# The count behind an order written by a planner: zeros' products booked as two instructions, a drift of the count, and a draw that passes attention products by

## The chip, the cores and the metric

The kernel runs on one core of a Trainium2 chip. The metric is the device time in microseconds of one execution.

## What is computed

Three stages follow each other; shapes are those of the run, all in fp32.

```python
# 1: delta-rule attention, 4 x 8 heads, 768 steps, head size 48
k_n = k / (norm(k) + 1e-6)
for t in range(768):
    y[t] = q[t] @ state
    state = state + beta[t] * outer(k_n[t], v[t] - k_n[t] @ state)
x = y as 3072 x 384
# 2: mixture of 8 experts, 384 -> 1024 -> 384, every token through every expert
P = exp(x @ w_gate - max)
for _ in range(8):
    P /= P.sum(1); P /= P.sum(0); P *= 3072 / 8
x = sum over e of P[:, e] * (relu(x @ w1[e]) @ w2[e])
# 3: a second layer
out = ((x @ w1) * (x @ w2)) @ w3 @ w_out
```

## The kernel before

The sequence is cut into 12 chunks of 64 steps. For each chunk the kernel forms products of the keys among themselves (the Gram matrices, tile `kt`), solves a triangular system on VectorE (`invert`, tiles `asys` and `t`), makes the transform `tt`, and walks from chunk to chunk with the state `st` (`seq`: products with `st`, `kt`, `qt`, `vs`, `u`, `pt`, `kraw`). A chunk has about 11 groups of such small fp32 products on TensorE; most are `quads` of 32 calls of `matmul`, booked with `ins=128` instructions, some are booked with 64. In the text these are the attention products. The result of a chunk goes to DRAM, comes back in another layout, and is split into a high and a low fp32r part, the tile `xr`.

Expert 0 of the mixture (`e0`) runs in the gaps of the attention: per chunk 24 groups of three matmuls with `xr` and 24 with the hidden layer `hA`, each booked with the default `ins=6`. It needs only the chunk's `xr`, of which there are two buffers. The weights of expert 0 lie in `wA`. Once the last chunk's gate logits are there, the eight rounds of normalisation of P run mostly on VectorE (`sinkhorn`). Then come experts 1 to 7 in three passes over the tokens (`unit`, tiles `xT`, `xr`, `wA`, `wS`, `hA`, `hB`); their weights go into the same buffers `wA` as expert 0's, so they can be written only when expert 0's products have read them. The last part is the second layer (`phase_c`).

The program is straight-line code. Its order is not written by hand: `Plan.order` is a list scheduler that runs when the program is built. It keeps a modelled clock `now`, takes the ready operations by priority, and gives each a start and an engine from a table of costs. The order in which it takes them is the order of the engines' queues; the hardware's own waits do the rest.

For TensorE the planner also keeps a model of where its code comes from. `issued` counts the instructions it has booked on TensorE so far, from the `ins` of each operation. In `fetch` the code is taken to come in blocks of `BLOCK = 256` instructions, with boundaries at `PHASE + 256 k` of that count, `PHASE = 193`; a block is taken to be ready `FETCH` microseconds after the first instruction of the block before it has started. `fetch(o, now)` is how long the operation `o` would then have to wait. In the choice (line 272) an operation of TensorE for which this is more than 0.1 us is put aside as `spare`, and the next in the list is looked at; it is taken after all when there is nothing else.

While the first chunk is on its way, TensorE would stand still. `setup` therefore books up to 400 products of zeros (line 497, tile `wz`, `fill=True`), which the planner uses only when nothing else is ready, from `WARM = 20` us of its clock until the first product of expert 0; the rest of them is then dropped. Each is booked with `ins=4`.

All matmuls are recorded in the profile under line 395, the helper `mm`, so they are told apart by their tiles.

Of the kernel before, what the change touches and what calls it, by code (L numbers as in the profile page):

```python
# [1 line left out]

# [75 lines left out]
class Plan:  # L78
# [52 lines left out]
    BLOCK = 256  # L131
    PHASE = 193
    AHEAD_AT = 0
    FETCH = 4.2
    SLOW = .06
    WARM = 20.0
    TURN = (.09, .1)

    def wait_for(self, o, e, pool, now, room):
# [10 lines left out]
    def order(self):  # L150
# [6 lines left out]
        now = 0.0  # L157
# [7 lines left out]
        issued = [3]  # L165
        last = ["e"]
        shared = {"DVE": 0.0, "POOL": 0.0}

        def cost_of(o, e):

            if e != "PE":
                return o.engs[e]
            k = int(now / win)
            if k not in warm:
                i = max(warm, default=-1)
                w = warm.get(i, False)
                while i < k:
                    b = busy.get(i, 0.0) / win
                    w = b >= .38 if w else b >= .7
                    i += 1  # L180
                warm[k] = w
            return (o.engs[e] + turn(o)) * (1.0 if warm[k] else self.COLD)

        def started(i, o, now):

            n = issued[0]
            if i >= n:
                return now + min(i - n, o.ins) / max(1, o.ins) * o.engs["PE"] + max(0, i - n - o.ins) * self.SLOW
            for i0, m, a, b in reversed(stream[-300:]):
                if i0 <= i < i0 + m:  # L190
                    return a + (b - a) * (i - i0) / m
            return 0.0

        def fetch(o, now):

            n = issued[0]
            k = -(-(n - self.PHASE) // self.BLOCK)
            b = self.PHASE + self.BLOCK * k
            ready = started(b - self.BLOCK + self.AHEAD_AT, o, now) + self.FETCH
            if b < n + o.ins:  # L200
                return max(0.0, ready - now - (b - n) / max(1, o.ins) * o.engs["PE"])
            if o.ins >= 16:
                return max(0.0, ready - now - o.engs["PE"] - (b - n - o.ins) * self.SLOW)
            return 0.0

        def turn(o):
            return self.TURN[0] if o.ins >= 16 and last[0] == "e" else self.TURN[1] if o.ins < 16 and last[0] == "a" else 0.0

        def crowded():

            return sum(max(0.0, b - max(a, now - win)) for a, b in lows[-8:]) > self.LOWMAX

        def room(o):
            t = o.est
            need = {}
            for s in o.slots:
                if s.at is not None:
                    continue
                g = s.ring
                if g.fifo and s.seq != g.given + need.get(("f", g), 0):  # L220
                    return None
                n = need.get(g, 0)
                if n >= len(g.free):
                    return None
                if s.cls in g.caps and g.used.get(s.cls, 0) + need.get((g, s.cls), 0) >= g.caps[s.cls]:
                    return None
                t = max(t, g.free[n][0])
                need[g] = n + 1
                need[("f", g)] = need.get(("f", g), 0) + 1
                need[(g, s.cls)] = need.get((g, s.cls), 0) + 1  # L230
            return t

        while pool:
# [4 lines left out]
            full = crowded()  # L238
            taken = set()
            lead = next((o for o in pool if o.fill), None)  # L240
            for o in pool:
                if o.fill and (now < self.WARM or o is not lead):
                    continue
                if o.est > now and len(taken) == len(free):
                    continue
                engs = [e for e in o.engs if free[e] <= now and o.rdy[e] <= now]
                if o.est > now:
                    nxt = o.est if nxt is None else min(nxt, o.est)
                    continue
                if not engs:  # L250
                    for e, t in o.rdy.items():
                        if t > now:
                            nxt = t if nxt is None else min(nxt, t)
                    continue
                t = room(o)
                if t is None:
                    continue
                if t > now:
                    nxt = t if nxt is None else min(nxt, t)
                    continue  # L260
                if len(o.engs) > 1:
                    cost = {x: max(free[x], o.rdy[x], now) + c * self.BIAS.get(x, 1.0) for x, c in o.engs.items()}
                    e = min(cost, key=cost.get)
                    if e not in engs:
                        t = max(free[e], o.rdy[e])
                        nxt = t if nxt is None else min(nxt, t)
                        continue
                else:
                    e = engs[0]
                if self.wait_for(o, e, pool, now, room):  # L270
                    continue
                if o.low and full or e == "PE" and fetch(o, now) > .1:
                    spare = spare or (o, e)
                    continue
                best = (o, e)
                break
            if best is None:
                best = spare
            if best is None:
                later = [t for t in free.values() if t > now] + ([self.WARM] if lead and now < self.WARM else []) + ([nxt] if nxt is not None else [])  # L280
                if not later:
                    raise RuntimeError("no operation can start: " + str([(o.prio, list(o.engs)) for o in pool[:8]]))
                now = min(later)
                continue
            o, e = best
# [14 lines left out]
            if e == "PE":  # L300
                late = fetch(o, now)
                end += late
                stream.append((issued[0], o.ins, now + late, end))
                last[0] = "a" if o.ins >= 16 else "e"
                issued[0] += o.ins
# [3 lines left out]
            elif e == "PE":  # L309
                t = now  # L310
                while t < end:
                    k = int(t / win + 1e-9)
# [60 lines left out]
class Kernel:  # L373
# [56 lines left out]
    def setup(self):  # L430
        nc, T, g = self.nc, self.T, self.g
        n = NCH * NG
# [61 lines left out]
        sw = self.psum.new("warm")  # L494
        for _ in range(400):
            g.op({"PE": .107}, lambda e: self.mm(self.ps(sw, 256), T["wz"][:, 0:128], T["wz"][:, 128:384], start=True, stop=True),
                 r=["wz"], w=[sw], ins=4, prio=1e6, fill=True)

    def vsrc(self, c):
        return self.a["v"][c]  # L500
# [1109 lines left out]
```

## Time and profile before

| | |
|---|---|
| median of 3 runs | 2100.17 us (2094.9 to 2104.77) |
| the profiled execution | 2098.94 us, its span 2097.1 us |
| instructions in the span | 40050 |
| TensorE (PE) busy | 2055.3 us, 98% of the span |
| VectorE (DVE), ScalarE (ACT), GpSimd (POOL) busy | 58%, 35%, 38% |
| mean granted clock of TensorE | 0.996 |

Times in the profile are microseconds from the start of the span. PE stands for TensorE's matmuls and PEld for its weight loads, which overlap them. Where a wait is called "issue", the engine waited for nothing that the profile shows. The queue "instruction" is one of the DMA queues of the core. The granted clock is a share of TensorE's full speed.

### The profile page before, as it was taken

The page shows a single profiled execution, that of the slowest core. Times are in us where ns is not written, and L with a number is a line of the kernel's source. Part 1 is how long each engine was busy: PE and PEld are TensorE (multiplying, and loading weights), DVE is VectorE, ACT ScalarE, POOL GpSimd, SP SyncE. Part 2 cuts the span into 40 slices and gives each one's busy share as a digit, 9 for nine tenths or more (in the row PEclk, how much of TensorE's full clock was granted, in tenths as well). Part 3 has the DMA queues.
Part 4 walks back from the last instruction along what each step waited for, and adds up shares of the span by engine and source line. Part 5 has one row for each costly group of instructions (what it writes and reads, how often), then busy time and mean ns, then how long its engine had stood idle before and what let it go on. Part 6 is the DMA issues. An engine that isn't in the chain of part 4 may idle for free.

```text
span 2097.1 us, 40050 instructions
## 1 busy us (share of the span) xinstructions
PE 2055.3 (98%) x16493; PEld 1758.3 (84%) x16493; DVE 1214.1 (58%) x1946; ACT 732.8 (35%) x1437; POOL 790.5 (38%) x851
## 2 busy tenths in 40 slices
PE   7998999999999999999999999999999999999999
PEld 6888888978888888878888888788888888988888
DVE  7889793466444445766666677676667643222222
ACT  6444433234334334323333324233233222222222
POOL 1200101037666667444654444444544534200000
PEclk9999999999999999999999999999999999999999
DMA  6443323256454465766656455655556547410000
GB/s 220 134 133 125 93 82 99 66 208 243 179 215 171 186 231 191 248 214 212 218 178 211 170 169 199 221 210 208 173 187 216 180 121 198 95 44 16 16 21 25
DMA packets 166615, 331.64 MB, mean 158 GB/s; under 512 B 13409, under 2 KB 117793, under 8 KB 154913
## 3 DMA queue, kind: packets, MB, share of 16 engines
q1 hardware_dynamic: 132544, 193.82, 27.3%
q0 software_dynamic: 33888, 135.28, 18.9%
q8 instruction: 129, 2.11, 0.4%
q14 instruction: 54, 0.43, 0.1%
HBM read 235.10 MB, written 93.95 MB: 157 GB/s over the span
## 4 chain that ended last, share of the span: by engine, by line
PE 75%; issue 5%; DMA 2%; POOL 1%; DVE 1%; ACT 0%; SPq 0%; POOLq 0%; DVEq 0%; ACTq 0%
PE b L395 75%; DMA acc<-y_d 1%; DMA rawB<-in_moe_w 1%; POOL wA L406 0%; POOL acc L406 0%; POOL sums L406 0%; DMA w_d<-cv 0%; DVE tmp L406 0%; DVE cv L406 0%; DVE cv L409 0%; DMA ws_d<-wS 0%; POOL wS L406 0%; ACT rt L399 0%; DVE rt L406 0%; DVE xr L406 0%
## 5 line engine op out<-in xcount | busy, mean ns | idle before, releaser
L395 PE MATMUL b<-hA,wA 128*128 128x512 f32 (+1 forms) x2367 | 507.7, 354 | 3.5 <-DVE hA L409 3.5
L395 PEld LDWEIGHTS b<-hA,wA 128*128 128x128 f32 x2367 | 393.6, 190 | 65.6 <-DVE hA L409 4.4
L406 POOL TENSOR_TENSOR acc<-acc,tmp 128x512 f32<-128x512 f32 x252 | 335.6, 1333 | 191.6 <-DVE tmp L406 189.9
L395 PE MATMUL b<-hB,wA 128*128 128x512 f32 x1521 | 386.0, 389 | 0.0
L395 PEld LDWEIGHTS b<-hB,wA 128*128 128x128 f32 x1521 | 285.5, 188 | 59.2
L395 PE MATMUL b<-xr,wA 128*128 128x256 f32 (+1 forms) x1620 | 329.8, 337 | 1.2 <-DVE hA L409 0.9
L395 PEld LDWEIGHTS b<-xr,wA 128*128 128x128 f32 x1620 | 252.2, 191 | 33.9 <-DVE hA L409 1.5
L399 ACT ACTIVATE rt<-b 128x512 f32<-128x512 f32 x300 | 178.8, 597 | 263.0 <-PE b L395 257.0
L395 PE MATMUL b<-xT,wA 128*128 128x512 f32 x1008 | 249.9, 389 | 1.3 <-POOL wA L406 1.1
L406 DVE TENSOR_TENSOR b<-b,rt 128x512 f32<-128x512 f32 x252 | 173.2, 695 | 107.1 <-ACT rt L399 75.8
L395 PEld LDWEIGHTS b<-xT,wA 128*128 128x128 f32 x1008 | 189.0, 188 | 41.2 <-POOL wA L406 2.1
L406 POOL TENSOR_TENSOR cv<-cv 128x256 f32<-128x256 f32 (+3 forms) x179 | 131.8, 736 | 205.2 <-DVE cv L1370 107.8
L395 PE MATMUL b<-xT,wS 128*128 128x512 f32 x756 | 199.9, 391 | 1.7 <-ACT rt L399 1.7
L406 DVE TENSOR_TENSOR tmp<-b,pb 128x512 f32<-128x512 f32 x150 | 103.2, 689 | 134.6 <-PE b L395 131.8
L409 DVE SCALAR_TENSOR_TENSOR hA<-b,hA 128x512 fp32r<-128x512 f32 x215 | 144.2, 688 | 61.1 <-ACT hA L935 29.8
L395 PEld LDWEIGHTS b<-xT,wS 128*128 128x128 f32 x756 | 142.2, 188 | 32.4 <-ACT rt L399 2.6
L406 DVE TENSOR_TENSOR rt<-b,rt 128x512 f32<-128x512 f32 x48 | 33.2, 692 | 186.0 <-PE b L395 186.0
L409 DVE SCALAR_TENSOR_TENSOR hB<-b,hB 128x512 fp32r<-128x512 f32 x169 | 114.7, 685 | 32.1 <-ACT hB L1175 31.6
L406 POOL TENSOR_TENSOR wA<-rawB,wA 128x768 fp32r<-128x768 f32 (+1 forms) x49 | 87.9, 1803 | 111.8 <-ACT wA L399 111.3
L406 DVE TENSOR_TENSOR tmp<-b,yr 128x512 f32<-128x512 f32 x102 | 70.2, 689 | 97.3 <-PE b L395 88.2
L1175 ACT ACTIVATE hB<-b 128x512 fp32r<-128x512 f32 x169 | 100.0, 595 | 67.7 <-DVE b L406 65.7
L399 ACT ACTIVATE cv<-cv 128x256 fp32r<-128x256 f32 x72 | 29.1, 404 | 266.7 <-DVE cv L409 266.7
(190 smaller groups left out, 2440.8 us busy)
## 6 DMA issues: line engine op xcount, KB each, us to landing
wA<-wq_d POOLq DMA_DIRECT2D x56, 1536.0 KB, 8.7
wq_d<-wA SPq DMA_DIRECT2D x28, 1536.0 KB, 7.0
wS<-ws_d POOLq DMA_DIRECT2D x56, 512.0 KB, 4.7
rawB<-in_moe_w SPq DMA_DIRECT2D x108, 192.0 KB, 3.3
ws_d<-wS SPq DMA_DIRECT2D x28, 512.0 KB, 6.8
w_d<-cv SPq DMA_DIRECT2D x112, 128.0 KB, 1.7
cvr<-in_w3T SPq DMA_DIRECT2D x32, 256.0 KB, 2.7
wS<-w_d POOLq DMA_DIRECT2D x32, 256.0 KB, 3.5
```

The costliest lines, as they stand in the source:

```text
L395: self.nc.tensor.matmul(*args, skip_group_check=True, **kw)
L399: self.nc.scalar.activation(out=out, in_=in_, func=AF.Copy, **({} if scale is None else {"scale": scale}))
L406: self.E[eng].tensor_tensor(out=out, in0=in0, in1=in1, op=op)
L409: self.nc.vector.scalar_tensor_tensor(out=out, in0=in0, scalar=scalar, in1=in1, op0=op0, op1=op1)
L1175: g.op({"ACT": actb(512)}, lambda e: nc.scalar.activation(out=hv(0), in_=self.ps(s, 512), func=AF.Relu), r=[s], w=[(out, 0, 0)], prio=pe)
```

## The change

Four things change in the planner's model, nothing in the operations themselves. A product of zeros counts as two instructions in place of four. The boundaries are no longer taken at `PHASE + 256 k` of the count alone: one further instruction is assumed for each 450 counted (`DRIFT`). The time that a block is taken to need rises from 4.2 to 4.4 us. And each time an operation of TensorE with 16 or more instructions (an attention product) would be chosen, a number is drawn from a generator with a fixed seed; in one case of twenty it is put aside like one whose code is late. The seed makes the order the same in every build.

```diff
+import random
...
-    FETCH = 4.2
+    FETCH = 4.4
+    DRIFT = 450
     SLOW = .06
     WARM = 20.0
+    SEED = 32
+    PASS_BY = .05
     TURN = (.09, .1)
...
         shared = {"DVE": 0.0, "POOL": 0.0}
+        rng = random.Random(self.SEED)
...
             n = issued[0]
-            k = -(-(n - self.PHASE) // self.BLOCK)
-            b = self.PHASE + self.BLOCK * k
+            extra = n // self.DRIFT
+            k = -(-(n + extra - self.PHASE) // self.BLOCK)
+            b = self.PHASE + self.BLOCK * k - extra
             ready = started(b - self.BLOCK + self.AHEAD_AT, o, now) + self.FETCH
...
-                if o.low and full or e == "PE" and fetch(o, now) > .1:
+                if o.low and full or e == "PE" and (fetch(o, now) > .1 or o.ins >= 16 and rng.random() < self.PASS_BY):
                     spare = spare or (o, e)
                     continue
...
             g.op({"PE": .107}, lambda e: self.mm(self.ps(sw, 256), T["wz"][:, 0:128], T["wz"][:, 128:384], start=True, stop=True),
-                 r=["wz"], w=[sw], ins=4, prio=1e6, fill=True)
+                 r=["wz"], w=[sw], ins=2, prio=1e6, fill=True)
```

## Rows read from the trace of the kernel before

**Rows 1.** Busy time of each engine, page of the profile.

```profile
PE 2055.3 (98%) x16493; PEld 1758.3 (84%) x16493; DVE 1214.1 (58%) x1946; ACT 732.8 (35%) x1437; POOL 790.5 (38%) x851
```

**Rows 2.** Busy us by stretch: window and length, then engines, clock, DMA.

```profile
75.00:355.00 280.00, 264.77 (x6873) 242.03 (x6870) 219.84 (x341) 115.62 (x268) 27.19 (x31) 0.98 0.35 105
355.00:436.00 81.00, 79.86 (x660) 78.66 (x659) 39.82 (x88) 24.04 (x47) 0.95 (x1) 1.00 0.23 70
436.00:2097.10 1661.10, 1648.25 (x7432) 1384.10 (x7430) 893.81 (x1416) 543.36 (x993) 743.64 (x799) 1.00 0.49 169
```

**Rows 3.** PE's waits from 75 to 355 us: total, times, longest.

```profile
PE b L395 <- issue: 9.2, 11, 1.6
```

**Rows 4.** PE's waits before 75 us.

```profile
PE b L395 <- issue: 2.9, 3, 1.2
```

**Rows 5.** PE's waits from 436 us to the end.

```profile
PE b L395 <- ACT rt L399: 4.4, 3, 2.7
PE b L395 <- DVE hA L409: 3.5, 2, 2.0
PE b L395 <- POOL wA L406: 1.1, 1, 1.1
```

**Rows 6.** The queue called instruction, DMA part of the page: packets, MB.

```profile
q8 instruction: 129, 2.11, 0.4%
```

**Rows 7.** Counts between ends of issue waits; PE counts matmuls, PEld loads.

```profile
13.89:39.72 25.83, 22.68 (x510) 18.63 (x510) 24.52 (x47) 21.93 (x73) 1.06 (x1) 1.00 0.58 206
...
210.64:240.21 29.57, 27.89 (x766) 25.46 (x766) 22.50 (x45) 11.24 (x27) 4.78 (x3) 1.00 0.31 91
240.21:245.68 5.47, 4.47 (x127) 4.18 (x128) 5.47 (x6) 4.73 (x11) 0.00 (x0) 0.64 0.48 150
...
13.89:331.25 317.36, 297.22 (x7656) 267.43 (x7655) 268.67 (x421) 148.72 (x364) 37.30 (x29) 0.98 0.38 117
```

**Rows 8.** Single blocks of code, cut at the same place of each.

```profile
35.09:39.72 4.63, 3.99 (x135) 3.61 (x132) 4.17 (x9) 1.07 (x2) 1.06 (x1) 1.00 0.89 278
...
113.12:115.21 2.09, 2.09 (x131) 2.03 (x131) 0.69 (x1) 1.28 (x4) 0.00 (x0) 1.00 0.60 221
...
142.09:145.92 3.83, 2.26 (x128) 1.90 (x127) 3.83 (x3) 2.32 (x7) 0.13 (x1) 1.00 0.45 131
...
302.43:305.92 3.49, 3.07 (x145) 2.72 (x136) 3.49 (x4) 1.08 (x2) 0.00 (x0) 1.00 0.30 76
```

**Rows 9.** The zeros (tile wz) from 15 to 75 us.

```profile
15.00:75.00 60.00, 28.92 (x220) 21.39 (x220) 0.00 (x0) 1.00 0.56 181
```

**Rows 10.** The two stretches at the lower granted clock (0.50).

```profile
146.20:149.60 3.40, 3.40 (x16) 3.40 (x17) 2.12 (x5) 0.83 (x2) 1.37 (x2) 0.50 0.89 258
...
241.80:252.00 10.20, 9.20 (x189) 8.78 (x193) 6.83 (x7) 6.18 (x14) 1.83 (x1) 0.50 0.29 79
```

**Rows 11.** Timeline of PE around 246 us: start, length, product, matmuls.

```profile
240.21 0.33 PE L395 MATMUL b<-vs,tt 64*64 64x48 f32 x6 [1.43 <-issue]
...
246.18 2.29 PE L395 MATMUL b<-xr,wA 128*128 128x256 f32 x9
248.27 2.76 PE L395 MATMUL b<-hA,wA 128*128 128x256 f32 x12
250.96 1.58 PE L395 MATMUL b<-pt,u 64*48 64x64 f32 x64
```

**Rows 12.** Timeline of PE around 332 us, at full clock.

```profile
327.89 0.62 PE L395 MATMUL b<-hA,wA 128*128 128x256 f32 x3
328.44 0.69 PE L395 MATMUL b<-asys,g 32*32 32x32 f32 x32
329.06 1.11 PE L395 MATMUL b<-pt,u 64*48 64x64 f32 x64
...
336.51 1.96 PE L395 MATMUL b<-hA,wA 128*128 128x256 f32 x15
338.40 1.15 PE L395 MATMUL b<-st,kt 48*64 48x48 f32 x64
```

## The prediction

> **What bounds the kernel now.** I begin with the page. PE is busy for 98% of the span, no other computing engine for more than 58% [rows 1]. Then I cut the span into stretches [rows 2]. The reader is to see there that from 75 us on PE is the limit everywhere: in the attention stretch (75 to 355 us) it is idle for 280.00 - 264.77 = 15.2 us, in the rest of expert 0 (355 to 436 us) for 1.1 us, and in everything after 436 us for 12.8 us of 1661. The list of what PE's idle time waited for comes next, stretch by stretch. From 75 to 355 us, 9.2 of the idle microseconds are called "issue": PE waited for nothing that the profile shows, 11 times [rows 3]. Before 75 us there are three more, 2.9 us together [rows 4]. After 436 us there is none; PE waits there for ScalarE, VectorE and GpSimd, 9.0 us in all [rows 5].
>
> What are the issue waits? The queue called "instruction" moved 129 packets and 2.11 MB, 16.4 KB each [rows 6]; PE ran 16493 matmuls and as many weight loads, 32986 instructions, which is 255.7 for each packet [rows 1, 6]. So PE's code comes in blocks of 256. Then I cut the span at the ends of the issue waits and counted matmuls and loads between them [rows 7]: 1020, 1532, 255 are three of the twelve counts, and all twelve are multiples of 256 less a few. From the end of the first wait (13.89 us) to that of the last (331.25 us) it is 15311 = 60 x 256 - 49. Every wait thus stands at the same place of a block, and the few that are missing (one in 312) are instructions of PE's queue that are not matmuls or loads. I read the waits as PE running off the end of a block before the next is there. A block lasts 317.36 / 60 = 5.3 us on average, and those that end in a wait last 3.5 to 5.5 us [rows 7, 8]; one of 2.09 us ended in none [rows 8], so what stood ahead of it counts too.
>
> **The change, part by part.**
>
> *The zeros' count.* 220 products of zeros were run, with 220 matmuls and 220 loads: two instructions each [rows 9]. The planner before booked four, so after the last of them (71 us) its count is 440 too high. In a block of 256 that sets its boundary 72 instructions behind the real one. The uncounted instructions push it on: after 49 of them it is some 120 behind, nearly half a block. The planner before did keep attention products away from boundaries, but from 15 us on from wrong ones. With two, its boundary is the real one less the uncounted instructions.
>
> *The drift.* One instruction in 450 books 15311 / 450 = 34 of those 49. The boundary is then at most some 15 instructions out by 331 us; an attention product of 128 takes 1.1 us [rows 12], so that is 0.13 us. Both edits together make the planner's boundaries right for the first time.
>
> *FETCH 4.2 to 4.4.* The planner holds an attention product back when the block would otherwise last less than this. I looked at eleven blocks that end in a wait; four of them stand in rows 7 and 8. They last from 3.49 to 5.47 us, and six of them longer than 4.4, by 2.4 us together: 0.22 us for each of the eleven. So with true boundaries a block that is planned tight still waits some 0.2 us. With 60 blocks of 5.3 us on average against 4.4, I take 16 as tight: 3.5 us stay. Bounds: none stays (0), or as many as now.
>
> *What a removed wait is worth.* Held-back attention leaves PE to expert 0's products; that work has to be done anyhow, and 80 us of it lie behind the attention's end [rows 2], so PE has something to run and each idle microsecond saved between 75 and 355 us brings the end of expert 0 forward by one. The work at 436 us hangs on that end: the next expert's weight tiles come free with its last products. VectorE is busy for 219.84 of the 280 us; if it set the pace of the attention, PE would still do expert 0's products in that time. The first wait (13.9 us, 1.2 us) stays: no zeros come before it. Of the other two before 75 us I count their 1.7 us, as the attention runs alone there. Removable: 9.2 + 1.7 = 10.9 us; less the 3.5 that stay, 7.4 us saved (bounds 0 and 10.9).
>
> *The clock.* In two stretches of the attention the granted clock is 0.50, which is 1.2 GHz in place of 2.4: 146.2 to 149.6 and 241.8 to 252.0 us [rows 10]. Each begins within 1.6 us of the end of an issue wait: the block up to 145.92 us is idle for its last 3.83 - 2.26 = 1.57 us [rows 8], and 1.43 us of waiting end at 240.21 [rows 11]. What they cost, from products at either level: at full clock 15 matmuls of expert 0 hold their place for 1.89 us, 0.126 each [rows 12]; in the slow stretch 9 and 12 take 2.09 and 2.69 us, 0.228 each [rows 11], so 0.45 of each slow us is lost. An attention product (b<-pt,u) takes 1.58 against 1.11 us: 0.30 lost [rows 11, 12]. The long stretch mixes both, with 9.2 us of work in its 10.2: at 0.40 it costs 3.7 us. The short one is nearly all expert 0: 1.5. If the fall follows the wait, both go; but another pause may bring another fall. I take 60% of the 5.2: 3.1 us saved (bounds: 5.2 saved; or as much again lost).
>
> *The draw.* Each time an attention product is the planner's choice it is put off by one turn with chance 1 in 20. By the code a chunk has about 11 such products, some 135 in all, so about 7 are put off, always behind something else that is ready. The work stays; what is added is a change between the two kinds. A single group of 3 expert-0 matmuls between attention products holds its place for 0.55 us where 3 in a row of 15 take 0.38 [rows 12]: 0.17 each, 1.2 us added (bounds 0 and 3; a gain through a luckier order is in the last item).
>
> *The rest of the order.* From 436 us on the same units run, but the planner's clock has shifted, so ties fall otherwise. The waits there are 9.0 us [rows 5]; I take no change, with bounds of 4 either way. The transfers and the other engines' work are the same.
>
> Sum: 2098.94 (the profiled execution; its span is 2097.1, 1.8 less) - 7.4 - 3.1 + 1.2 = 2089.6. The runs' median is 2100.17, 1.2 above the profiled one; I forecast for that median: **2090.8 us**, 0.45% less. A measurement of this kernel tells about 0.5% (10.5 us) from no change, as its three runs span 9.9 us, so the forecast lies next to that edge.
>
> **The rivals.**
>
> *The waits stay, or move (no change).* The boundaries are right, yet held-back attention piles up and runs two products deep right behind the boundary, and the next block is short. For it: a block with a wait starts the next late too (the blocks up to 240.21 and 245.68 both wait [rows 7, 8]), and 5.3 us on average leaves only 0.9 us of room. Against it: most of the 60 blocks have no wait even with wrong boundaries. Time: 2100.2 + 1.2 for the draw, less 0 to 4 of waits: about 2099.
>
> The Trainium skill (Runtime: NRT & Kernel Launch, section Instruction fetch mechanics) says that the sequencer fetches the next 16 KiB page while it runs the current one, and that crossing a boundary is mostly hidden. By that rule the edits would gain nothing, and the time would be that of this rival; the trace disagrees for the attention, with 12.1 us in 14 waits, and agrees after 355 us, where there is none.
>
> *Everything goes (clearly faster).* No wait but the first (-10.9), both slow stretches (-5.2), draws free, 2 us less waiting in the last part: 2100.2 - 18.1 = 2082. For it: slow stretches began behind waits. Against: the planner's price is an average over blocks that differ by 2 us.
>
> *The clock falls more often (slower).* The new order makes other pauses between 75 and 355 us, and the granted clock falls at them. Price 0.40 us for each slow us. Without any clock gain the sum is 2100.2 - 7.4 + 1.2 = 2094; to be slower by 10.5 us it takes 17 us more, 42 us of further slow clock, four stretches as long as the worst now. Against it: 13.6 us in all are slow there, with 14 waits.
>
> **How the numbers follow.** Chances: forecast 0.58 (2083 to 2098, which the edge of 2089.7 cuts nearly in half: faster 0.28, same 0.30); waits stay 0.20 (same); everything goes 0.14 (faster); clock 0.08 (slower). That is faster 0.42, same 0.50, slower 0.08. The range leaves out the slower case and the lower part of "everything goes", and takes in the bounds of the draw and of the last part: 2080 to 2101.
>
> **What the profile after will show.** Right: the issue waits of PE before 355 us fall from 12.1 to about 4.7 us (3.5 and the first); what is left still stands at multiples of 256; the clock is 1.00 from 75 to 355 us but for at most one stretch; expert 0's last product ends 7 to 13 us before 436; the stretch after takes 1661 us as before, give or take 4. Wrong: as many issue waits as now (the boundary or the 4.4 us are not what decides), or the waits gone and the same microseconds found as waits for VectorE or ScalarE (the attention, not PE, set the pace), or more of the span at 0.50.

## The result and the profile after

The changed kernel takes 2076.44 us (median of 4 runs, 2073.56 to 2079.21) against 2097.53 for the kernel before: 0.9896 of it, with a 95% interval of 0.9862 to 0.9931. The forecast was 2090.8 with a range of 2080 to 2101; the gain is 21 us where 9 were forecast, and the time lies under the range. The profiled execution has a span of 2076.4 us.

First the stretches, cut where expert 0's last product ends: at 436.4 us before, at 414.9 us after. The columns are those of [rows 2]; the first fence is of the kernel before, the second of the changed one.

```profile
0.00:436.40 436.40, 407.46 (x9066) 374.61 (x9067) 320.65 (x531) 189.85 (x446) 47.29 (x53) 0.98 0.37 117
436.40:2097.10 1660.70, 1647.85 (x7428) 1383.69 (x7427) 893.41 (x1416) 542.96 (x992) 743.25 (x799) 1.00 0.49 169
```

```profile
0.00:414.90 414.90, 394.38 (x9036) 365.51 (x9037) 317.88 (x534) 190.62 (x447) 48.55 (x51) 1.00 0.39 123
414.90:2076.40 1661.50, 1649.69 (x7428) 1384.33 (x7426) 890.99 (x1414) 542.47 (x992) 743.80 (x799) 1.00 0.49 169
```

The reader is to see that all of the gain lies in the first row. It is 21.5 us shorter, and the rest of the kernel takes 1661.5 us against 1660.7. Of the 21.5 us, 8.4 are idle time of PE (436.4 - 407.46 = 28.9 before, 414.90 - 394.38 = 20.5 after) and 13.1 are busy time, though the same products of attention and of expert 0 run.

Next the stretch before 75 us, of the kernel before and of the changed one, then the attention stretch of [rows 2] and the zeros, both of the changed kernel.

```profile
0.00:75.00 75.00, 62.42 (x1542) 53.51 (x1543) 60.58 (x103) 49.79 (x131) 18.74 (x21) 1.00 0.62 211
```

```profile
0.00:75.00 75.00, 60.28 (x1559) 52.16 (x1560) 58.16 (x101) 47.17 (x123) 23.46 (x23) 0.98 0.58 201
75.00:355.00 280.00, 275.33 (x6997) 255.34 (x6995) 222.58 (x350) 124.05 (x288) 23.71 (x27) 1.00 0.37 112
```

```profile
15.00:75.00 60.00, 24.64 (x189) 17.83 (x186) 0.00 (x0) 0.97 0.50 168
```

From 75 to 355 us PE is idle for 4.7 us where it was for 15.2 [rows 2], and the granted clock is 1.00 where it was 0.98. From 15 to 75 us the zeros take 24.6 us in place of 28.9 [rows 9], but this is not time gained: PE's idle time before 75 us rises from 12.6 to 14.7 us, and the first product of expert 0 starts at 63.1 us where it started at 64.0.

The waits of PE, before 75 us and from 75 to 355 us, as in [rows 3, 4]:

```profile
PE b L401 <- DVE u L412: 2.5, 1, 2.5
PE b L401 <- DVE tt L412: 2.4, 1, 2.4
...
PE b L401 <- issue: 0.8, 1, 0.8
```

```profile
PE b L401 <- issue: 1.9, 2, 1.7
PE b L401 <- ACT u L405: 1.6, 1, 1.6
```

Issue waits are 2.7 us in 3 places where they were 12.1 in 14. The one long one that is left, in the timeline:

```profile
237.89 0.56 PE L401 MATMUL b<-kt 48*64 48x64 f32 x18
240.18 0.86 PE L401 MATMUL b<-kt 48*64 48x64 f32 x44 [1.73 <-issue]
```

One stretch before the end of expert 0 still has the lower clock, 30.7 to 34.1 us, and it begins 1.1 us after the end of a wait of 2.42 us for VectorE:

```profile
29.65 1.16 PE L401 MATMUL b<-tt,xst 64*64 64x64 f32 x64 [2.42 <-DVE tt L412]
30.75 0.40 PE L401 MATMUL b<-wz 128*128 128x256 f16 x1
31.07 1.96 PE L401 MATMUL b<-vs,tt 64*64 64x48 f32 x64
```

```profile
30.70:34.10 3.40, 3.40 (x79) 2.74 (x72) 3.40 (x7) 3.33 (x11) 0.00 (x0) 0.50 0.02 5
```

### The profile page after: what moved, and what is told of

It reads as the page before. It is cut to its first block, busy times and chain, and to the rows that moved or that the text cites. A ratio compares the mean times of both kernels' runs of the same rounds, so it can differ in the third digit from the quotient of the medians.

```text
span 2076.4 us, 39969 instructions
## 1 busy us (share of the span) xinstructions
PE 2044.1 (98%) x16463; PEld 1749.8 (84%) x16463; DVE 1208.9 (58%) x1947; ACT 733.1 (35%) x1438; POOL 792.4 (38%) x849
## 4 chain that ended last, share of the span: by engine, by line
PE 87%; DVE 5%; DMA 5%; issue 1%; POOL 1%; ACT 1%; SPq 0%; POOLq 0%; DVEq 0%; ACTq 0%
PE b L401 87%; DMA acc<-y_d 1%; DMA wo_d<-cv 1%; DVE prod L412 1%; DMA xs_d<-xst 1%; DMA xst<-xs_d 0%; DMA rawB<-in_moe_w 0%; SPq L432 0%; DMA xT<-xs_d 0%; DVE cv L415 0%; POOL acc L412 0%; DVE xs L625 0%; POOL wA L412 0%; DVE hA L415 0%; DMA xf_d<-acc 0%
```

## The experiments

Two theories stood against each other. By the boundary theory the gain comes from code boundaries that the planner now places rightly, so that fewer attention products run into a block that is not there. By the luck theory the draw, or the shaking of the order by any edit, happened on a good order. Each run was timed beside the kernel before, and each ratio is to that; "issue" is the issue waits of PE up to the end of expert 0, "slow" the time up to there at which the granted clock was 0.50 (1.2 GHz), both from the trace of one execution, and the last column is where expert 0's last product ends in it. The traced execution is not always near the median: that of e11 took 2094.56 us, that of e12 2087.52.

| run | median us | ratio, 95% interval | issue us | slow us | expert 0 ends |
|---|---|---|---|---|---|
| before | 2097.53 | 1 | 12.1 | 13.7 | 436.4 |
| changed | 2076.44 | 0.9896 (0.9862 to 0.9931) | 2.7 | 3.4 | 414.9 |
| e1 count alone | 2091.65 | 0.9975 (0.9960 to 0.9989) | 4.2 | 13.7 | 434.2 |
| e2 no draw | 2080.32 | 0.9916 (0.9891 to 0.9941) | 3.7 | 10.2 | 422.0 |
| e3 draw alone | 2094.58 | 0.9984 (0.9967 to 1.0000) | 10.6 | 27.3 | 439.6 |
| e4 planner half a block off | 2088.24 | 0.9947 (0.9925 to 0.9969) | 4.6 | 30.7 | 432.5 |
| e5 count and drift | 2080.04 | 0.9908 (0.9887 to 0.9928) | 4.3 | 6.8 | 420.3 |
| e6 4.4 us alone | 2095.46 | 0.9990 (0.9975 to 1.0005) | 7.3 | 17.1 | 435.2 |
| e7 seed 33 | 2085.12 | 0.9932 (0.9907 to 0.9957) | 2.1 | 13.7 | 426.7 |
| e8 seed 1 | 2096.31 | 0.9996 (0.9980 to 1.0012) | 6.7 | 30.7 | 438.2 |
| e12 seed 2 | 2092.87 | 0.9991 (0.9974 to 1.0008) | 1.5 | 27.3 | 431.5 |
| e17 no draw, drift 312 | 2076.63 | 0.9913 (0.9893 to 0.9932) | 2.4 | 3.4 | 421.1 |
| e18 no draw, 5.2 us | 2114.59 | 1.0095 (1.0072 to 1.0117) | 0.9 | 44.4 | 454.2 |
| e9 changed, code moved 128 | 2078.20 | 0.9912 (0.9889 to 0.9934) | 2.9 | 0 | 416.0 |
| e13 changed, code moved 64 | 2083.81 | 0.9939 (0.9919 to 0.9960) | 4.8 | 17.1 | 423.2 |
| e14 changed, code moved 192 | 2078.11 | 0.9904 (0.9886 to 0.9922) | 2.9 | 6.8 | 416.7 |
| e16 no draw, code moved 128 | 2087.93 | 0.9954 (0.9938 to 0.9970) | 4.9 | 17.1 | 432.1 |
| e11 count and drift, code moved 128 | 2088.58 | 0.9966 (0.9952 to 0.9980) | 8.7 | 17.1 | 434.7 |
| e10 before, code moved 160 | 2085.55 | 0.9957 (0.9942 to 0.9973) | 4.0 | 10.2 | 426.2 |
| e15 before, code moved 48 | 2091.60 | 0.9972 (0.9962 to 0.9982) | 6.6 | 17.1 | 437.1 |

**One edit at a time.** The count alone:

```diff
# kernel before
-                 r=["wz"], w=[sw], ins=4, prio=1e6, fill=True)
+                 r=["wz"], w=[sw], ins=2, prio=1e6, fill=True)
```

> Kernel before with one edit: a product of zeros counts as two instructions. Boundary theory (the gain comes from block boundaries that the planner places rightly): without the drift its boundaries are right to within 10 instructions at 90 us and 49 at 331 us, so most of the gain comes with this edit alone: issue waits of PE before 355 us down from 12.1 to 3 to 6 us, time 2080 to 2088 us. Luck theory (the drawn order is simply a good one; the count decides nothing): 12 us of issue waits as before, time within 6 us of the kernel before.

A quarter of a per cent, 6.6 us: between the two forecasts, just outside the 6 us allowed for no change. The issue waits did fall as the boundary theory said, from 12.1 to 4.2 us. But expert 0 ends only 2 us earlier, since PE's other waits grew by 8.6 us. Waits of this run, before 75 us:

```profile
PE b L395 <- ACT vs L399: 3.8, 1, 3.8
```

The wait of 3.8 us ends at 62.8 us, and at 62.9 the clock falls for 10.2 us. So a removed issue wait is not a gained microsecond by itself; what matters is the sum of PE's pauses and what the clock does after them.

The draw taken out of the changed kernel, and the draw alone put into the kernel before (shown as what it amounts to, without the constants):

```diff
# e2: changed kernel
-    PASS_BY = .05
+    PASS_BY = 0.0
# e3: kernel before
+        rng = random.Random(self.SEED)
...
-                if o.low and full or e == "PE" and fetch(o, now) > .1:
+                if o.low and full or e == "PE" and (fetch(o, now) > .1 or o.ins >= 16 and rng.random() < self.PASS_BY):
```

> Changed kernel without the draw (its chance is 0): count, drift and 4.4 us stay. Boundary theory: issue waits about 3 us, as in the changed kernel with 2.7, and a time within 5 us of it, 2072 to 2082 us. Luck theory: the draw carries the gain, so 2090 us or more.

> Kernel before with the draw alone (same seed, four instructions for a zeros' product, no drift, 4.2 us). Boundary theory: the boundaries are as wrong as before, so issue waits of 10 to 14 us and a time within 6 us of the kernel before. Luck theory: a good part of the gain, 2088 us or less.

Both came out as the boundary theory said: 2080.3 us without the draw, and 2094.6 with nothing but the draw, with 10.6 us of issue waits.

Count and drift without the 4.4 us and the draw, and the 4.4 us alone:

```diff
# e5: changed kernel
-    FETCH = 4.4
+    FETCH = 4.2
-    PASS_BY = .05
+    PASS_BY = 0.0
# e6: kernel before
-    FETCH = 4.2
+    FETCH = 4.4
```

> Changed kernel without the draw and with the time of a block at 4.2 us as before: count and drift alone. If right boundaries carry the gain (boundary theory), issue waits stay at 3 to 5 us and the time at 2078 to 2084 us, near the 2080.3 of the kernel without the draw. If the longer 4.4 us carries it (rate theory: a planner that spaces attention products further apart meets fewer late blocks, wherever it puts the boundaries), issue waits of 6 us or more and 2088 us or more, near the 2091.7 of the count alone.

> Kernel before with the time of a block at 4.4 us, nothing else. Boundary theory: boundaries as wrong as before, 10 us or more of issue waits, 2092 to 2102 us. Rate theory: issue waits fall to about 5 us as in the run with boundaries half a block off (4.55 us), and 2085 to 2090 us.

2080.0 and 2095.5 us: count and drift carry 0.92% by themselves, the 4.4 us nothing that can be told from no change (the interval of e6 holds 1), with or without right boundaries. The issue waits of e6 were a miss: 7.3 us, less than either 10 or the 12.1 of the kernel before, at boundaries as wrong as there. The drift alone, with four instructions for a product of zeros, was not run.

**The place of the boundary, by the planner.** All boundaries of the planner moved by half a block, the draw kept:

```diff
# e4: changed kernel
-    PHASE = 193
+    PHASE = 65
```

> Changed kernel with the first boundary at 65 in place of 193: every boundary of the planner half a block off, all else kept, the draw too. Boundary theory: issue waits come back to 10 us or more before 355 us, each still at a multiple of 256 instructions from the others, and the time to 2092 to 2104 us. Luck theory: another order, so anything from 2076 to 2100 us, and issue waits that bear no relation to the place of the boundary.

Faster than the boundary theory allowed, 2088.2 us, and its issue waits are only 4.6 us. That part of the theory fell: wrong boundaries do not always bring the waits back. The time is 12 us above the changed kernel all the same, and 30.7 us at the lower clock go with it.

**The place of the boundary, by the code.** A cleaner test keeps the order to the letter and moves the real boundaries: tiny products of zeros, two instructions each, go ahead of PE's first product, where it waits for its first keys anyhow.

```diff
     for o in order:
+        if o.eng == "PE":
+            for _ in range(ahead):   # e9, e11, e16: 64; e10: 80; e13: 32; e14: 96; e15: 24
+                self.mm(self.bank[7][0:32, 0:16], self.T["wz"][0:32, 0:32], self.T["wz"][0:32, 128:144], start=True, stop=True)
+            ahead = 0
         o.fn(o.eng)
```

> Changed kernel, its order of operations kept to the letter, with 64 tiny products of zeros (128 instructions) put ahead of PE's first product, where PE waits for its first keys until 4.1 us anyhow. The real boundaries of the code move by half a block against the same order. Boundary theory: issue waits before 355 us rise from 2.7 to 7 us or more, and the time from 2076 to 2084 us or more. Luck theory (this order is good for other reasons): issue waits below 4 us and 2074 to 2080 us.

> The kernel with count and drift alone (2080.0 us, 4.4 us of issue waits), its order kept, and 64 tiny products of zeros (128 instructions) ahead of PE's first: half a block off. Boundary theory: issue waits of 8 us or more and 2086 us or more. Luck theory: 2078 to 2083 us.

> Changed kernel without the draw (2080.3 us, 3.7 us of issue waits), its order kept, with 64 tiny products of zeros (128 instructions) ahead of PE's first. Boundary theory, as the run with count and drift alone bore it out (8.7 us, 2088.6 us): 7 us or more of issue waits and 2086 us or more. If orders with count, drift and 4.4 us are even, below 5 us and 2077 to 2083 us.

For the two orders without a draw the place counts. Count and drift alone lose 8.5 us when the code moves by half a block under them (2080.0 to 2088.6, intervals that do not touch), with issue waits of 8.7 us in place of 4.3; the order without the draw at 4.4 us loses 7.6 (its intervals overlap by a hair), though its issue waits rise only from 3.7 to 4.9 us, short of the 7 expected. That the waits are bound to the code and not to the order shows when matmuls and loads are counted from the start of the span to the end of one wait each, in the kernel before, in e15 (the same order with 48 instructions in front) and in e11 (128 in front):

```profile
0.00:142.08 142.08, 127.52 (x3286) 112.97 (x3287) 119.07 (x193) 76.31 (x192) 21.98 (x25) 1.00 0.50 164
```

```profile
0.00:144.78 144.78, 127.42 (x3286) 111.62 (x3287) 117.77 (x190) 75.77 (x191) 22.50 (x25) 0.98 0.48 157
```

```profile
0.00:142.20 142.20, 124.79 (x3286) 110.94 (x3286) 110.83 (x180) 77.49 (x197) 24.66 (x26) 0.96 0.49 163
```

6573, 6573 and 6572, with the instructions in front counted in. It is so everywhere: all 119 issue waits of the twenty traces end within 6 instructions of 193 + 256 k, if one uncounted instruction is allowed for each 312. The changed kernel's own order, however, lost nothing by half a block, as the luck theory said: 2078.2 us and 2.9 us of waits. Was that a chance?

> Changed kernel, order kept, 32 tiny products of zeros (64 instructions, a quarter of a block) ahead of PE's first. If this order is even enough to run under any boundary (as half a block suggests: 2.9 us of issue waits, 2078.2 us), issue waits stay below 4 us and the time at 2074 to 2081 us. If half a block was a chance, 6 us of waits and 2083 us or more.

> Changed kernel, order kept, 96 tiny products of zeros (192 instructions, three quarters of a block) ahead of PE's first: as for a quarter; 2074 to 2081 us and below 4 us of issue waits if the order is even, 2083 us or more if not.

Three quarters of a block cost nothing either (2078.1), a quarter 7 us (2083.8, intervals that overlap). So this order is more even than the others, but perhaps not under every boundary. And 64 or 96 of the tiny products by themselves cost nothing in this order.

> Kernel before, its order kept to the letter, with 80 tiny products of zeros (160 instructions) ahead of PE's first product. The planner of before put its boundaries 72 (after the last zero) to 121 instructions (at 331 us) behind the real ones, which is 184 to 135 ahead of the next; 160 instructions in front bring the real ones to within 25 of them, without a change of the order. Boundary theory: issue waits fall from 12.1 to 5 us or less, the slow stretches behind them go, and the time falls by 6 to 14 us, to 2084 to 2092 us. Luck theory: no change, 2094 to 2102 us.

> Kernel before, order kept, 24 tiny products of zeros (48 instructions) ahead of PE's first: control for the run with 80, which gained 9 us. The planner's boundaries are now 120 to 169 instructions from the real ones, so further off than before. If the place of the boundary made that gain, nothing is gained here: 10 us or more of issue waits, 2092 to 2104 us. If the tiny products themselves made it (a start in the higher clock, say), 2084 to 2090 us here too.

Moved to where its planner had put the boundaries, the kernel before gains 9 us and keeps 4.0 of 12.1 us of issue waits, with no change of its order. But the control, whose boundaries are further off than in the kernel before, gains 6 us as well, with 6.6 us of issue waits: neither forecast, and its interval overlaps that of e10. The kernel before thus stood at a bad place, and how much of the 9 us is due to the boundaries being right these two runs do not settle.

What right boundaries do shows when the 70 blocks up to the end of expert 0 are timed by that count, their waits taken off. PE runs through 12 of them in less than 3.5 us in the kernel before, and through 1 in the changed one. Over all runs it is 0 to 6 of them where the planner's boundaries are right, 6 in e1, and 9 to 15 where they are wrong, but for e14 with 4. The short blocks go with the boundaries, then; the time does so only in part.

**The draw.** Only the seed changes:

```diff
# e7, e8, e12: changed kernel
-    SEED = 32
+    SEED = 33   # e8: 1; e12: 2
```

> Changed kernel with the next seed, 33. If the draw only shakes the order, the time lies near that without a draw, 2080 us, by 6 us either way, with issue waits of 2 to 5 us. If the seed 32 is a chosen one, this one is slower than it by 4 us or more.

> Changed kernel with seed 1: as for seed 33. Both seeds at 2080 us or above speak for a lucky seed 32; one below 2076 us and one above speaks for plain scatter.

> Changed kernel with seed 2. With seeds 32, 33 and 1 at 2076, 2085 and 2096 us and 2080 us without a draw, plain scatter puts this at 2076 to 2096 us. If it is above 2080 us, the draw costs on average and seed 32 is a fortunate one.

2085.1, 2096.3 and 2092.9 us, against 2080.3 without a draw: seeds 1 and 2 are slower than no draw at all, by 16 and 13 us, and seed 33 by 5, within the intervals. Of four seeds 32 is the only one below the kernel without a draw: a fortunate one. Boundaries that the planner places rightly thus do not make a fast order by themselves, as all four seeds have them. Seed 2 has just 1.5 us of issue waits, fewer than the changed kernel, and is still 16 us slower; the stretches of this run show where:

```profile
75.00:355.00 280.00, 270.62 (x6635) 248.24 (x6634) 218.82 (x340) 115.91 (x271) 20.19 (x21) 0.96 0.31 97
```

The granted clock is 0.96 from 75 to 355 us against 1.00, and 27.3 us up to the end of expert 0 run at 1.2 GHz. That is no single trace's chance: the 11 executions of this order have a mean granted clock of 0.993, the four of the changed kernel 0.9975.

**What is left to set.** The drift that the trace of before shows, one in 312, and a longer time for a block:

```diff
# e17: changed kernel
-    DRIFT = 450
+    DRIFT = 312
-    PASS_BY = .05
+    PASS_BY = 0.0
# e18: changed kernel
-    FETCH = 4.4
+    FETCH = 5.2
-    PASS_BY = .05
+    PASS_BY = 0.0
```

> Changed kernel without the draw (2080.3 us) and with one further instruction for each 312 counted, the share that the trace of before showed, in place of 450. If the 15 instructions of remaining error matter, issue waits fall below 3 us and the time to 2074 to 2079 us. If the rest of the gain is chance of the order, 2076 to 2090 us, not tied to the issue waits but to the time at the lower clock and the other waits.

> Changed kernel without the draw (2080.3 us) and with 5.2 us for a block in place of 4.4. If issue waits still cost what they seem, they fall to the first one alone (below 2 us) and the time by 1 to 3 us, 2076 to 2080 us. If the planner then has to hold attention products for too long, waits for other engines and zeros' products take over: 2084 us or more.

With the traced drift and no draw the kernel takes 2076.6 us, as the changed one does with its draw; the 3.7 us to e2 lie within the intervals. The longer time is the most telling miss. The issue waits go down to the first one, 0.9 us, and the kernel is the slowest of all, 2114.6 us:

```profile
75.00:355.00 280.00, 258.98 (x6246) 237.85 (x6245) 215.84 (x332) 106.76 (x249) 15.28 (x16) 0.93 0.31 95
```

```profile
PE b L401 <- DVE hA L415: 3.7, 5, 1.3
PE b L401 <- DVE tt L412: 3.1, 2, 2.6
...
```

PE is idle for 21 us from 75 to 355 us, none of it for code; it waits mostly for VectorE and ScalarE, and 44.4 us run at the lower clock. I read it as these engines getting the attention's products too late; no run tests that. None of the runs beats the changed kernel by more than the runs differ.

## Why the prediction was wrong

**What bounds the kernel** held: the issue waits stand at code boundaries (the counts of the experiments' section show them at one place of a block in every trace), and the gain ended up entirely before the end of expert 0, with 1661.5 us after it against 1660.7.

**The zeros' count and the drift** carry the change, as said, and together: 0.92% (e5). The drift was described as a small thing worth 0.13 us at the boundary. That is so for the step from 34 to 49 instructions, but without any drift (e1) 0.25% is left. Whether the 49 instructions or another chance order did that, one run does not tell.

**FETCH** was worth nothing alone (e6) nor beside the count and the drift (e2 against e5).

**The step that failed is the sum.** Up to the end of expert 0 it had 9.3 us; the two traces differ by 21.5. (1) "3.5 us stay" was too much: of the 10.9 us called removable 1.9 stayed, and the first wait shrank by 0.4, so the issue waits gave 9.4 us and not 7.4. The price of 0.22 us is an average in which one block has 1.07 of the 2.4 us, the one of 5.47 us that began at the end of a wait [rows 7]; with true boundaries the 16 blocks taken as tight did not wait that much. (2) PE's other idle time between 75 and 355 us, 15.2 - 9.2 = 6.0 us, was put at nothing without a word. It fell to 2.8, so all idle time there fell by 10.5 us. At the start, also put at nothing, little came of it: the zeros took 3.7 us less in all, and PE's idle time other than issue grew by 4.2 us before 75 us. Idle time and zeros together are 12.1 us of the 21.5. (3) "I take 60%" of the slow stretches: from 75 to 355 us both went, and one of 3.4 us came at 30.7. At the prediction's own prices that is 5.2 less 1.4, or 3.8 us between these two traces, against 3.1. (4) The draw's 1.2 us did not show with seed 32 (2076.4 against 2080.3 without, within the intervals); two of the other seeds cost over ten times as much, so what a draw costs is not a few changes between products. These terms make 15.9 us. The other 5.6 us or so are products that take less time in the records at the same granted clock. Changes between attention, zeros and expert 0's two kinds of products do not explain it, with 314 of them before and 319 after; the cause stays open.

**That the clock term came near was luck.** It took the two slow stretches of one execution as belonging to the order. The mean granted clock is known for 97 executions of the kernel before, timed beside the experiments: it goes from 0.993 (median 2102 us) to 1.000 (2089 us) under one and the same order. Their mean is 0.9967, that of the four of the changed kernel 0.9975; at the 13 us that lie between 0.993 and 1.000 this is some 1.5 us, an estimate. At an equal clock the gain is still there: at 0.997 the kernel before takes 2096.3 us (median of 25) and the changed one 2078.2 and 2079.2; at 0.998 it is 2094.9 (of 20) against 2073.6 and 2074.7. So 17 us or more of the 21 are not the clock.

That runs with little slow time (0 to 7 us) end expert 0 by 421.1 us and those with 27 us or more at 431.5 us or later does not show that waits and clock go together: 27 us at 1.2 GHz are 11 to 12 us by themselves at the prices of 0.40 to 0.45, and e12 has 1.5 us of issue waits with 27.3 slow. The rival in which everything goes came nearest, with 2082, but part of that is luck too: it counted 2 us less waiting in the last part, where the time grew by 0.8.

**The rivals.** That the waits stay or move is what happens with seed 1, with 6.7 us of issue waits, and with a block of 5.2 us, where they become waits for other engines. That the clock falls more often is shown by e18, which is slower by 0.95%: issue waits gone, 44.4 us slow. The rule of the Trainium skill that a boundary is mostly hidden (Runtime: NRT & Kernel Launch, section Instruction fetch mechanics) held after expert 0, where no trace has an issue wait, and not in the attention, where moving the code by half a block under an unchanged order cost 8.5 us (e11).

**What stays open.** With the planner's boundaries right (the changed kernel, e2, e5, e7, e8, e10, e12, e17, e18) the issue waits are 0.9 to 6.7 us, 3.1 on average; with wrong ones (the kernel before, e3, e4, e6, e9, e11, e13 to e16) 2.9 to 12.1, 6.5 on average. The times are less clear: right boundaries without a draw gave 2076.6, 2080.0 and 2080.3 us, but 2114.6 with a block of 5.2 us and 2085 to 2096 with three seeds; wrong ones, with the code not moved, 2088.2 (e4) to 2097.5. (e1, right only at first, is in neither group.) About 8 us hang on the place of the boundary itself in two orders (e11, clearly; e16, at the edge of its intervals), though both also run at the lower clock for a while before 60 us, 10.2 us in e11 and 6.8 in e16, where the same orders without the products in front do so not at all (e5) or for 3.4 us (e2); some of the loss may be that. In the changed kernel's order nothing clear hangs on the place: 2 us (e9, e14) and 7 (e13), all within the intervals. The rest goes with the order, by its other waits and slow stretches; that a planner with right boundaries makes better orders is only argued, from three of them, and the seeds speak against it as a rule. The last 4 us of the changed kernel over e2 lie within the intervals.

## What to carry to other kernels

Where a planner orders the instructions, compare its own counts with the trace: two windows cut at the ends of unexplained waits showed the block, and one tile's count the wrong price of two instructions for four. Before the slow stretches of one trace are priced as a gain, compare the granted clock of all executions of the kernel: here 13 us went with it under one and the same order. Ask of all idle time of the bounding engine what becomes of it, not only of the part that the change aims at. Before a random draw is credited, run three other seeds and no draw.

## What the runs showed of the hardware

In these traces TensorE's code came in blocks of 256 instructions (129 packets for 32986), and where the kernel before ran through one in 3.5 to 5.5 us it could end in a wait, of up to 1.7 us in the two kernels. The place of the waits moved with the code when 48 or 128 instructions were put in front: the counts of 6573, 6573 and 6572 above. After some pauses (1.43 and 1.57 us in the kernel before, 2.42 in the changed one, 3.8 in e1) the granted clock stood at 1.2 GHz for 3.4 to 10.2 us, while another of that length, the 1.73 us at 240 us in the changed kernel, was followed by no such stretch. Nor does each fall follow a long pause: in e3 the clock fell at 219.8 us, for 3.4 us, with no pause of 0.3 us since 213.9. One order, that of the kernel before, had mean granted clocks from 0.993 to 1.000 in 97 executions.
